# Four accumulators in turn for the first expert layer, and the written order on three engines

## The chip, the cores and the metric

The kernel runs on one core of a Trainium2 chip. The metric is the device time of one execution in microseconds (us). Three runs of the kernel before took 635.12, 649.59 and 657.23 us; their median, 649.59 us, is the time before. The profiled execution is a fourth one and took 627.53 us.

## The reference

Two blocks follow each other, all in 32-bit floats.

```
state = gamma * state + k_t v_t^T ;  y_t = scale * q_t state      # retention: batch 4, 8 heads, 768 steps, width 64
x = y as (3072 tokens, 512)
expert = argmax(x @ w_gate) ;  gate = its softmax weight           # 8 experts
out[token] = gate * ( relu(x[token] @ w1[expert]) @ w2[expert] )   # w1: 512 x 1024, w2: 1024 x 512
```

No token is dropped: each expert takes as many tokens as chose it.

## The kernel before

**Retention.** 24 steps (6 chunks of 128 positions for 4 batches) make the tokens, their logits and, chunk by chunk, the place of each token in its expert's list. Tokens are written to DRAM (`x_d`).

**Early block.** Behind the last retention step, the first 256 tokens of expert 0 go through both layers (`layer1(EARLY, ...)`, `layer2(EARLY, ...)`, lines 420 to 429), with the last logits and the placing of the last chunk (the generator `rest`) woven in between. PE's order there is the written one.

**Counts.** A matmul (`cnt`, line 434) counts the tokens of each expert. Vector instructions (lines 437 to 445) make of each count an arm number: the number of tokens is rounded up to a multiple of 32, and each multiple from 128 to 512 has code of its own, an arm.

**Jobs.** Each expert e is a job (line 469). A register on each engine that takes part holds the job's arm number; `tc.Switch` (line 479) jumps to that arm, and at the arm's end the engine jumps out again. PE and ScalarE (ACT) have arms in every job, GpSimd (POOL) in the last alone. In an arm:
- `layer1` is called for f = 0 to 7. Each call has PE gather 4 matmuls in one PSUM accumulator (`hp`), and ScalarE takes it to SBUF with a Relu (line 189). The accumulator's tag is `"sc"`, which has 2 buffers. A third call must wait until ScalarE has emptied the first accumulator.
- `turn` transposes the next job's tokens (4 tiles, tag `"tr"`, 3 buffers), and ScalarE copies them out.
- `layer2` multiplies by the second weights, tile by tile of 128 tokens (tag `"y"`, 2 buffers), ScalarE copies each result out (line 202). The last, partial tile goes first.

Between the arms, GpSimd scatters the job's 4 result tiles to the output (line 206) and gathers the tokens for the job after next (line 151), and SyncE loads the weights for the job after next (2 MB each for `w1t` and `w2t`, lines 140 and 141).

**What sets the order.** In the early block PE, and in the jobs PE and ScalarE, follow the written order (`tc.manual_schedule`). All else is placed by a scheduler: it moved all 8 register loads (`regs`, line 465) of PE and of ScalarE ahead of the first job (three of ScalarE's stand between the early block's last two Relus), moved `cnt` to the middle of the early block, and mixed GpSimd's scatters and gathers of neighbouring jobs.

**PSUM tags.** `"sc"` 2 buffers, `"tr"` 3, `"y"` 2, `"lg"` 1. In the retention part `"lg"` holds the logits, and after it `cnt`.

Of the kernel before, what the change touches and what calls it, by code (L numbers as in the profile page):

```python
# [12 lines left out]
F32 = mybir.dt.float32  # L13
I32 = mybir.dt.int32
# [3 lines left out]
ALU = mybir.AluOpType  # L18
AX = mybir.AxisListType

P = 128
# [29 lines left out]
def kernel(  # L51
# [11 lines left out]
    nc = tc.nc  # L63
    B, H, S, D = q.shape
    N, DM = out.shape
    E = w_gate.shape[1]
# [4 lines left out]
    DT = DM // P  # L71
    FT = F // P
    W = 512
    TC = W // P
    EARLY = 256
# [9 lines left out]
    def ps(tag, bufs, name):  # L85
        return psum.tile([P, 512], F32, tag=tag, name=name, bufs=bufs)
# [25 lines left out]
    def rt(shape, name, dt=F32):  # L112
        return route.tile(shape, dt, tag=name, name=name)
# [23 lines left out]
    def weights(pool, e):  # L137
        w1t = pool.tile([P, 1, DT, F], F32, tag="w1t", name="w1t")
        w2t = pool.tile([P, 1, FT, DM], F32, tag="w2t", name="w2t")
        nc.sync.dma_start(w1t, w1v[:, ds(e, 1), :, :])  # L140
        nc.sync.dma_start(w2t, w2v[:, ds(e, 1), :, :])
        return w1t, w2t

    first = ctx.enter_context(tc.tile_pool(name="first", bufs=1))
    xs2 = [first.tile([P, TC, DM], F32, tag=f"xs{i}", name=f"xs{i}") for i in range(2)]
# [3 lines left out]
    def gather(xs, idx, tiles, rows=N):  # L149
        for t in tiles:  # L150
            nc.gpsimd.indirect_dma_start(  # L151
                out=xs[:, t, :], out_offset=None, in_=x_d[0:rows, :],
                in_offset=bass.IndirectOffsetOnAxis(ap=idx[:, t : t + 1], axis=0), bounds_check=rows - 1,
                oob_is_err=False)
# [22 lines left out]
    def turn(xs, xT, tiles, evict):  # L177
        for t in tiles:
            tr = ps("tr", 3, "trs").rearrange("p (a t) -> p a t", a=DT)
            for dt in range(DT):  # L180
                nc.tensor.transpose(tr[:, dt, :], xs[:, t, ts(dt, P)], ident)
            evict(out=xT[:, :, ts(t, P)], in_=tr)

    def layer1(n, xT, w1t, hT, f):
        hp = ps("sc", 2, "hp")[:, 0:n]
        for dt in range(DT):
            nc.tensor.matmul(hp, lhsT=w1t[:, 0, dt, ts(f, P)], rhs=xT[:, dt, 0:n], start=(dt == 0),  # L187
                             stop=(dt == DT - 1))
        nc.scalar.activation(out=hT[:, f, 0:n], in_=hp, func=AF.Relu)  # L189

    def layer2(n, hT, w2t, o, t):

        m = min(n - t * P, P)
        parts = P // m if m in (P // 4, P // 2) else 1
        y = ps("y", 2, "ye")
        c = DM // parts
        for f in range(FT):
            for j in range(parts):
                nc.tensor.matmul(y[j * m : j * m + m, 0:c], lhsT=hT[:, f, t * P : t * P + m],  # L199
                                 rhs=w2t[:, 0, f, ts(j, c)], start=(f == 0), stop=(f == FT - 1))  # L200
        for j in range(parts):
            nc.scalar.copy(out=o[0:m, t, ts(j, c)], in_=y[j * m : j * m + m, 0:c])  # L202

    def scatter(o, idx, tiles):
        for t in tiles:
            done = nc.gpsimd.indirect_dma_start(  # L206
                out=out[:, :], out_offset=bass.IndirectOffsetOnAxis(ap=idx[:, t : t + 1], axis=0), in_=o[:, t, :],
                in_offset=None, bounds_check=N - 1, oob_is_err=False)

            tc.declare_no_dep(done.ins, group="scatters", reason="other rows of the output")  # L210
            tc.add_to_no_dep_group("scatters", done.ins)


    with ExitStack() as actx:
# [191 lines left out]
        for n in range(len(steps)):  # L406
# [6 lines left out]
            last, done = done, retain(n)  # L413
# [6 lines left out]
        with tc.manual_schedule(engines={mybir.EngineType.PE}):  # L420
            turn(xs2[0], xTa, range(EARLY // P), nc.vector.tensor_copy)
            for f in range(FT):
                layer1(EARLY, xTa, wa[0], hTa, f)
                if f != 4:
                    next(rest, None)
            for _ in rest:
                pass
            for t in range(EARLY // P):
                layer2(EARLY, hTa, wa[1], oa, t)
# [5 lines left out]
    ne = rt([P, E], "ne")  # L435
    arm = rt([P, E], "arm", I32)
    nc.vector.tensor_copy(ne, cnt)

    STEP, LEAST, MOST = 32, P // 32, W // 32
# [8 lines left out]
    PE, ACT, POOL = mybir.EngineType.PE, mybir.EngineType.Activation, mybir.EngineType.Pool  # L448


    mp = ctx.enter_context(tc.tile_pool(name="mp", bufs=2))
    keep2 = ctx.enter_context(tc.tile_pool(name="keep2", bufs=1))
    o2 = [keep2.tile([P, TC, DM], F32, tag=f"o{i}", name=f"o{i}") for i in range(2)]
    for t in o2:
        nc.vector.memset(t, 0.0)
    sets = [wa, weights(keep2, 1)]
    cols = [(src_i[:, ts(e, TC)], dst_i[:, ts(e, TC)]) for e in range(E)]
    HALF = EARLY // P

    gather(xs2[1], cols[0][0], range(HALF, TC))  # L460
    gather(xs2[0], cols[1][0], range(TC))
    xT = mp.tile([P, DT, W], F32, tag="xTs", name="xTs")
    turn(xs2[1], xT, range(HALF, TC), nc.vector.tensor_copy)

    def regs(e, engines):
        return {g: nc.engines[g].value_load(arm[0:1, e : e + 1], min_val=0,
                                            max_val=MOST - LEAST - (EARLY // STEP if e == 0 else 0)) for g in engines}

    for e in range(E):
        w1t, w2t = sets[e]  # L470
        skip = EARLY if e == 0 else 0
        arms = MOST - LEAST + 1 - skip // STEP
        engines = [PE, ACT] + ([POOL] if e == E - 1 else [])
        which = regs(e, engines)
        if e + 1 < E:
            xTn = mp.tile([P, DT, W], F32, tag="xTs", name="xTs")
        hT = mp.tile([P, FT, W], F32, tag="hT", name="hT", bufs=1)
        with tc.manual_schedule(engines={PE, ACT}):
            for a in tc.Switch(which, arms):
                n = STEP * (LEAST + a)  # L480
                for f in range(FT):
                    layer1(n, xT[:, :, skip:], w1t, hT, f)
                if e + 1 < E:
                    turn(xs2[e % 2], xTn, range(TC), nc.scalar.copy)
                tiles = -(-n // P)
                for t in [tiles - 1] + list(range(tiles - 1)):
                    layer2(n, hT, w2t, o2[e % 2], t)
                    if e == E - 1:
                        scatter(o2[e % 2], cols[e][1], [t])
        if e + 1 < E:  # L490
            tiles = range(TC - HALF) if e == 0 else range(TC)
            scatter(o2[e % 2], cols[e][1][:, HALF:] if e == 0 else cols[e][1], tiles)
            xT = xTn
        if e + 2 < E:
            gather(xs2[(e + 1) % 2], cols[e + 2][0], range(TC))
            sets.append(weights(first if e % 2 == 0 else keep2, e + 2))


    most = rt([P, 1], "most")
    over = rt([P, 1], "over", I32)  # L500
    nc.vector.tensor_reduce(most, ne, axis=AX.X, op=ALU.max)
    nc.vector.tensor_scalar(out=over, in0=most, scalar1=float(W), scalar2=None, op0=ALU.is_gt)
    more = nc.values_load(over[0:1, 0:1], min_val=0, max_val=1)
    with tc.If(more > 0), tc.tile_pool(name="op", bufs=1) as op:

# [51 lines left out]
        for j in range(OV):  # L557
            ev = nc.sync.value_load(whose[0:1, j : j + 1], min_val=0, max_val=E - 1)
            w1t, w2t = weights(keep2, ev)
            gather(xs2[j % 2], osrc_i[:, ts(j, TC)], range(TC))  # L560
            xT = mp.tile([P, DT, W], F32, tag="xTs", name="xTs")
            hT = mp.tile([P, FT, W], F32, tag="hT", name="hT", bufs=1)
            turn(xs2[j % 2], xT, range(TC), nc.vector.tensor_copy)
            for f in range(FT):
                layer1(W, xT, w1t, hT, f)
            for t in range(TC):
                layer2(W, hT, w2t, o2[j % 2], t)
            scatter(o2[j % 2], odst_i[:, ts(j, TC)], range(TC))
# [25 lines left out]
```

## Time and profile before

| | us |
|---|---|
| median of 3 runs (lowest, highest) | 649.59 (635.12, 657.23) |
| profiled execution, its span | 627.53, 625.7 |
| retention and early block, to the first job | about 227 |
| jobs 0 to 7, first matmul to last | 227.5 to about 610 |
| behind the last matmul | about 15 |
| PE busy | 563.8 (90%) |
| ScalarE busy | 123.8 (20%) |

The sizes of the jobs that the trace shows: job 0 runs 128 further tokens, jobs 1, 2, 5 and 7 the arm for 416, job 3 for 448, job 4 for 352, job 6 for 384. A 32-bit matmul stands in the trace as two pieces, so that a call of `layer1` is 8 pieces and two calls are the "x16" of a row. Times in rows count from the start of the span. A bracket at a row's end gives how long the engine sat idle before it and what ended that. "issue" means that the profile shows nothing that the engine waited for.

### The profile page before, as it was taken

The numbers are of one execution on the slowest core, as the hardware profiler recorded it, in microseconds if no ns is written. First come the engines' busy times: TensorE is split into PE (matmuls) and PEld (weight loads), VectorE is DVE, ScalarE is ACT, GpSimd is POOL, SyncE is SP. The second block draws the span as 40 slices with busy tenths as digits, with TensorE's granted clock in tenths as the row PEclk, the third lists the DMA queues.
The fourth block names the chain that finished last, engine by engine and source line by source line (L and its number), as shares of the span: only waits on it lengthen the run. The fifth ranks groups of instructions, "written<-read, shape, count | busy, mean of one in ns | idle before, by whom it ended". The sixth has DMA issues, their size and how long they took to land.

```text
span 625.7 us, 7784 instructions
## 1 busy us (share of the span) xinstructions
PE 563.8 (90%) x3160; PEld 371.6 (59%) x3160; DVE 108.5 (17%) x291; ACT 123.8 (20%) x245; POOL 118.8 (19%) x156
## 2 busy tenths in 40 slices
PE   4999999999999988799799989969979996999990
PEld 4988989898988664364355445436435543545540
DVE  2445555466453220000000000000000000000000
ACT  2223232323232211130012012002001201201100
POOL 8331312222220433002102200210310010000011
PEclk9997979899999999899899979999998997999996
DMA  9964647956120449513504410450550314000011
GB/s 186 211 126 124 137 129 213 316 124 159 34 89 14 132 125 381 192 47 137 186 0 170 134 75 18 170 187 0 190 183 0 139 43 147 0 4 20 4 37 50
DMA packets 96476, 72.50 MB, mean 116 GB/s; under 512 B 77946, under 2 KB 77946, under 8 KB 96384
## 3 DMA queue, kind: packets, MB, share of 16 engines
q1 hardware_dynamic: 88096, 52.46, 31.4%
q0 software_dynamic: 5120, 12.60, 5.9%
q10 hardware_dynamic: 3168, 6.29, 2.7%
q8 instruction: 48, 0.79, 0.6%
q14 instruction: 44, 0.36, 0.2%
HBM read 60.84 MB, written 14.68 MB: 121 GB/s over the span
## 4 chain that ended last, share of the span: by engine, by line
issue 56%; PE 28%; POOL 8%; DVE 4%; DMA 1%; POOLq 1%; SPq 0%; DVEq 0%
PE y L288 7%; POOL out_dram L206 4%; PE sc L260 4%; POOL xs L151 4%; PE tr L246 4%; PE y L284 4%; PE lg L308 3%; PE new L269 2%; PE hp L187 2%; PE trx L303 2%; DVE am L262 1%; DMA q<-in_q_dram 1%; DVE xT L305 0%; DVE state L276 0%; SPq L232 0%
## 5 line engine op out<-in xcount | busy, mean ns | idle before, releaser
L187 PE MATMUL hp<-xTs,w1t 128*128 128x416 f32 (+4 forms) x512 | 177.9, 509 | 31.5 <-ACT hT L189 27.8
L187 PEld LDWEIGHTS hp<-xTs,w1t 128*128 128x128 f32 x512 | 98.4, 204 | 111.4 <-issue 66.5
L199 PE MATMUL ye<-w2t,hT 128*128 128x512 f32 (+3 forms) x640 | 164.0, 455 | 0.0
L199 PEld LDWEIGHTS ye<-w2t,hT 128*128 128x128 f32 (+3 forms) x640 | 74.8, 155 | 84.2 <-issue 83.2
L206 POOL DMA_INDIRECT out_dram<-o,dst x30 | 29.8, 995 | 294.3 <-ACT o L202 236.7
L189 ACT ACTIVATE hT<-hp 128x416 f32<-128x416 f32 (+4 forms) x64 | 30.0, 480 | 178.5 <-PE hp L187 123.7
L288 PE MATMUL y<-vs,am 128*128 128x64 f32 x384 | 59.8, 276 | 1.6 <-DVE am L262 0.9
L288 PEld LDWEIGHTS y<-vs,am 128*128 128x128 f32 x384 | 54.5, 202 | 4.5 <-issue 1.8
L202 ACT COPY o<-ye 128x512 f32<-128x512 f32 (+3 forms) x40 | 17.7, 444 | 144.6 <-PE ye L199 144.3
L151 POOL DMA_INDIRECT xs<-x_d,src x30 | 30.3, 1009 | 72.6 <-PE ye L199 35.5
L262 DVE TENSOR_TENSOR am<-sc,causal 128x512 f32<-128x512 f32 x48 | 31.3, 685 | 41.7 <-PE sc L260 41.7
L284 PE MATMUL y<-stb,qT 128*128 128x128 f32 x160 | 37.6, 319 | 0.0
L260 PE MATMUL sc<-qT,kT 64*128 64x128 f32 x384 | 36.3, 300 | 0.9 <-DVE am L262 0.9
L279 POOL COPY stb<-state 64x256 f32<-64x256 f32 x40 | 19.6, 490 | 80.0 <-DVE state L276 78.9
L241 POOL TENSOR_TENSOR vs<-v,dec 128x512 f32<-128x512 f32 x24 | 25.4, 1062 | 38.5 <-PE new L269 25.7
L260 PEld LDWEIGHTS sc<-qT,kT 64*128 64x128 f32 x384 | 28.9, 196 | 5.2 <-issue 4.2
L291 ACT COPY xg<-y 128x512 f32<-128x512 f32 x24 | 14.1, 589 | 84.4 <-PE y L288 84.4
L284 PEld LDWEIGHTS y<-stb,qT 128*128 128x128 f32 x160 | 25.6, 202 | 1.3
L246 PE MATMUL tr<-ident,qs 128*128 128x128 f32 x96 | 18.5, 318 | 7.0 <-DVE qs L240 7.0
L308 PE MATMUL lg<-wg,xT 128*128 128x8 f32 x192 | 24.5, 254 | 0.3
L308 PEld LDWEIGHTS lg<-wg,xT 128*128 128x128 f32 x192 | 23.4, 192 | 1.7 <-DVE xT L305 1.2
L248 ACT COPY qT<-tr 128x512 f32<-128x512 f32 x24 | 14.1, 587 | 37.6 <-PE tr L246 37.6
(111 smaller groups left out, 340.4 us busy)
## 6 DMA issues: line engine op xcount, KB each, us to landing
w1t<-in_moe_w_dram SPq DMA_DIRECT2D x8, 2048.0 KB, 8.0
w2t<-in_moe_w_dram SPq DMA_DIRECT2D x8, 2048.0 KB, 12.0
q<-in_q_dram SPq DMA_DIRECT2D x24, 256.0 KB, 4.6
k<-in_k_dram SPq DMA_DIRECT2D x24, 256.0 KB, 3.2
v<-in_v_dram SPq DMA_DIRECT2D x24, 256.0 KB, 4.4
x_d<-xg ACTq DMA_DIRECT2D x6, 1024.0 KB, 4.4
xs<-x_d,src POOLq DMA_INDIRECT x30, 3.5
out_dram<-o,dst POOLq DMA_INDIRECT x30, 7.1
```

The source lines that it names most:

```text
L151: nc.gpsimd.indirect_dma_start(out=xs[:, t, :], out_offset=None, in_=x_d[0:rows, :], in_offset=bass.IndirectOffsetOnAxis(ap=idx[:, t : t + ...
L187: nc.tensor.matmul(hp, lhsT=w1t[:, 0, dt, ts(f, P)], rhs=xT[:, dt, 0:n], start=(dt == 0), stop=(dt == DT - 1))
L189: nc.scalar.activation(out=hT[:, f, 0:n], in_=hp, func=AF.Relu)
L199: nc.tensor.matmul(y[j * m : j * m + m, 0:c], lhsT=hT[:, f, t * P : t * P + m], rhs=w2t[:, 0, f, ts(j, c)], start=(f == 0), stop=(f == FT ...
L206: done = nc.gpsimd.indirect_dma_start(out=out[:, :], out_offset=bass.IndirectOffsetOnAxis(ap=idx[:, t : t + 1], axis=0), in_=o[:, t, :], i ...
L241: nc.gpsimd.tensor_tensor(out=vs, in0=vt, in1=inner(gk, D), op=ALU.mult)
L246: nc.tensor.transpose(tr[:, a, :], src[:, 2 * a : 2 * a + 2, :].rearrange("p h d -> p (h d)"), ident)
L260: nc.tensor.matmul(sc[j][:, a, :], lhsT=kT[r, a, :], rhs=qT[r, a, :], start=True, stop=True)
L262: nc.vector.tensor_tensor(out=am[j], in0=sc[j], in1=middle(causal[:, :], HP), op=ALU.mult)
L284: nc.tensor.matmul(y[:, ts(a, P)], lhsT=qT[:, a, :], rhs=stb[b][c % 2][:, a, :], start=True, stop=False, skip_group_check=True)
L288: nc.tensor.matmul(y[:, ts(h, D)], lhsT=am[j][:, a, :], rhs=vs[:, h, :], start=(c == 0), stop=True, skip_group_check=True)
L308: nc.tensor.matmul(lg[:, b, :], lhsT=xT[:, dt, :], rhs=wg[:, dt, :], start=(dt == 0), stop=(dt == DT - 1))
```

## The change

It does four things. `layer1` takes its accumulators in turn from 4 places: two of `"sc"`, then `"lg"`, then one of `"tr"`; this holds for the early block too, which calls the same function. The jobs, the gathers ahead of them and the first `turn` now stand in one block in which PE, ScalarE and GpSimd keep the written order. The register for job e + 1 is loaded just ahead of job e's switch (that for job 0 ahead of the first `turn`). The two vector instructions for `most` and `over` move ahead of the jobs.

```diff
+    hp_tags = [("sc", 2), ("sc", 2), ("lg", 1), ("tr", 3)]
     def layer1(n, xT, w1t, hT, f):
-        hp = ps("sc", 2, "hp")[:, 0:n]
+        hp = ps(*hp_tags[f % len(hp_tags)], "hp")[:, 0:n]
...
+    with tc.manual_schedule(engines={PE, ACT, POOL}):
+        gather(xs2[1], cols[0][0], range(HALF, TC))
+        gather(xs2[0], cols[1][0], range(TC))
+        which = regs(0)
+        xT = mp.tile([P, DT, W], F32, tag="xTs", name="xTs")
+        turn(xs2[1], xT, range(HALF, TC), nc.vector.tensor_copy)
+        for e in range(E):
...
+            if not last:
+                nxt = regs(e + 1)
...
-        with tc.manual_schedule(engines={PE, ACT}):
-            for a in tc.Switch(which, arms):
+            for a in tc.Switch(which, arms_of(e)):
                 n = STEP * (LEAST + a)
...
+            if not last:
+                scatter(o2[e % 2], cols[e][1][:, HALF:] if e == 0 else cols[e][1], range(TC - HALF if e == 0 else TC))
+                xT, which = xTn, nxt
+            if e + 2 < E:
+                gather(xs2[(e + 1) % 2], cols[e + 2][0], range(TC))
+                sets.append(weights(first if e % 2 == 0 else keep2, e + 2))
```

The order of the built programs at three places follows (a row is a line, an operation, what it writes and reads, and its size; "x" counts equal ones in a row; lines behind 183 are 2 to 9 higher in the changed kernel).

**PE, from the middle of the early block to the first job.** `found` places the last tokens, `hp` and `ye` are the early block's two layers, `trs` is the first `turn`. Before:

```order
L368 MATMUL found<-val,here 128x64
L434 LDWEIGHTS ones_b
L434 MATMUL cnt<-acc,ones_b 128x8
L187 MATMUL hp<-xTa,w1t 128x256 x8
L199 MATMUL ye<-w2t,hTa 128x512 x16
L181 MATMUL trs<-ident,xs_104 128x128 x8
L466 TENSOR_LOAD arm
L466 ISA x2
```

Seven more pairs of these two rows follow, and then the switch and the first job. Changed:

```order
L370 MATMUL found<-val,here 128x64
L189 MATMUL hp<-xTa,w1t 128x256 x8
L201 MATMUL ye<-w2t,hTa 128x512 x16
L436 LDWEIGHTS ones_b
L436 MATMUL cnt<-acc,ones_b 128x8
L471 TENSOR_LOAD arm
L471 ISA x2
L181 MATMUL trs<-ident,xs_104 128x128 x8
L471 TENSOR_LOAD arm
L471 ISA x2
L594 SWITCH_STRIDE
```

`cnt` has moved behind the whole second layer, and a register load that needs its result stands ahead of the transposes; two loads are left of eight.

**PE, the first layer in the arm for 416 tokens of job 1,** with the engines whose semaphores an instruction waits for. Before:

```order
L187 MATMUL hp_3924<-xTs_2457,w1t_2404 128x416 x3
L187 MATMUL hp_3930<-xTs_2457,w1t_2404 128x416 x4
L187 MATMUL hp_3936<-xTs_2457,w1t_2404 128x416 [waits Activation_49]
L187 MATMUL hp_3936<-xTs_2457,w1t_2404 128x416 x3
L187 MATMUL hp_3942<-xTs_2457,w1t_2404 128x416 [waits Activation_49]
```

Changed:

```order
L189 MATMUL hp_3943<-xTs_2481,w1t_2404 128x416 x3
L189 MATMUL hp_3949<-xTs_2481,w1t_2404 128x416 x4
L189 MATMUL hp_3955<-xTs_2481,w1t_2404 128x416 x4
L189 MATMUL hp_3961<-xTs_2481,w1t_2404 128x416 [waits PE_49]
L189 MATMUL hp_3961<-xTs_2481,w1t_2404 128x416 x3
L189 MATMUL hp_3967<-xTs_2481,w1t_2404 128x416 [waits Activation_49]
```

The first wait for ScalarE stood at the third call and now stands at the fifth.

**GpSimd, the end of the jobs.** `o` is a result tile, `xs` a gathered one. Before, jobs 5 and 6 and the entry of the last:

```order
L206 DMA out_dram<-o_2401,dst 3072x512 x2
L590 UNCONDITIONAL_BRANCH
L206 DMA out_dram<-o_2401,dst 3072x512 x2
L206 DMA out_dram<-o_2400,dst 3072x512 x2
L590 SWITCH_STRIDE
```

Changed, from the gathers behind job 5:

```order
L151 DMA xs_103<-x_d,src 128x512 x4
L471 TENSOR_LOAD arm
L471 ISA x2
L594 UNCONDITIONAL_BRANCH
L208 DMA out_dram<-o_2400,dst 3072x512 x4
L594 SWITCH_STRIDE
```

All four scatters of job 6 now stand ahead of the last switch, where two of them stood behind the last job; and each job's four gathers stand behind its four scatters, at the boundary between two jobs.

## Rows read from the trace of the kernel before

**Rows 1.** The page, costliest groups: out<-in, count | busy us, mean ns | idle before, releaser.

```profile
L187 PE MATMUL hp<-xTs,w1t 128*128 128x416 f32 (+4 forms) x512 | 177.9, 509 | 31.5 <-ACT hT L189 27.8
```

**Rows 2.** Waits from 240 us on: engine, line, releaser: total us, times, longest.

```profile
ACT hT L189 <- issue: 54.8, 6, 11.0
...
PE hp L187 <- issue: 2.0, 1, 2.0
```

**Rows 3.** Timeline of PE, 240 us on: start, duration, line, operation, count, idle before.

```profile
255.75 18.60 PE L187 MATMUL hp<-xTs,w1t 128*128 128x416 f32 x48 [4.39 <-ACT hT L189]
...
308.41 19.57 PE L187 MATMUL hp<-xTs,w1t 128*128 128x416 f32 x48 [4.02 <-ACT hT L189]
...
362.00 21.36 PE L187 MATMUL hp<-xTs,w1t 128*128 128x448 f32 x48 [3.56 <-ACT hT L189]
...
409.37 4.90 PE L187 MATMUL hp<-xTs,w1t 128*128 128x352 f32 x16
419.60 16.03 PE L187 MATMUL hp<-xTs,w1t 128*128 128x352 f32 x48 [5.34 <-ACT hT L189]
...
457.84 5.75 PE L187 MATMUL hp<-xTs,w1t 128*128 128x416 f32 x16
468.22 19.88 PE L187 MATMUL hp<-xTs,w1t 128*128 128x416 f32 x48 [4.63 <-ACT hT L189]
...
512.39 5.32 PE L187 MATMUL hp<-xTs,w1t 128*128 128x384 f32 x16
522.79 18.62 PE L187 MATMUL hp<-xTs,w1t 128*128 128x384 f32 x48 [5.08 <-ACT hT L189]
...
570.11 17.03 PE L187 MATMUL hp<-xTs,w1t 128*128 128x416 f32 x48 [0.74 <-ACT hT L189]
```

**Rows 4.** Timeline of ScalarE: the first Relus of jobs 4, 5, 6 and 7.

```profile
419.09 0.82 ACT L189 ACTIVATE hT<-hp 128x352 f32<-128x352 f32 x2 [8.93 <-issue]
...
467.65 0.93 ACT L189 ACTIVATE hT<-hp 128x416 f32<-128x416 f32 x2 [9.02 <-issue]
...
522.25 0.87 ACT L189 ACTIVATE hT<-hp 128x384 f32<-128x384 f32 x2 [9.08 <-issue]
...
569.54 0.93 ACT L189 ACTIVATE hT<-hp 128x416 f32<-128x416 f32 x2 [5.14 <-PE hp L187]
```

**Rows 5.** Windows: stretch, length, busy time of five engines, granted clock, DMA share, GB/s.

```profile
298.60:308.40 9.80, 5.79 (x17) 2.85 (x15) 0.00 (x0) 1.14 (x3) 3.02 (x3) 0.92 0.85 272
308.40:314.00 5.60, 5.59 (x9) 2.94 (x10) 0.00 (x0) 0.37 (x1) 0.00 (x0) 0.54 0.12 44
563.60:570.20 6.60, 5.86 (x18) 2.94 (x16) 0.00 (x0) 1.25 (x3) 0.98 (x1) 1.00 0.13 47
```

**Rows 6.** Timeline of ScalarE, the early block's last Relu, right behind three register loads.

```profile
212.36 0.38 ACT L189 ACTIVATE hTa<-hp 128x256 f32<-128x256 f32 x1 [1.35 <-issue]
```

**Rows 7.** Timeline of PE and VectorE, 200 to 228 us.

```profile
200.08 3.70 PE L187 MATMUL hp<-xTa,w1t 128*128 128x256 f32 x16
207.40 0.17 PE L434 MATMUL cnt<-acc,ones_b 128*128 128x8 bf16 x1
224.70 1.04 PE L181 MATMUL trs<-ident,xs 128*128 128x128 f32 x8
227.47 7.38 PE L187 MATMUL hp<-xTs,w1t 128*128 128x128 f32 x64 [1.73 <-DVE xTs L182]
...
200.49 0.19 DVE L320 TENSOR_TENSOR dl<-lg,mx 128x32 f32<-128x32 f32 x1
209.04 0.14 DVE L445 TENSOR_SCALAR arm<-arm 128x1 int32<-128x1 int32 x1
```

**Rows 8.** Timeline of GpSimd at the end.

```profile
610.72 0.98 POOL L206 DMA_INDIRECT out_dram<-o,dst  x1 [5.88 <-ACT o L202]
614.01 0.98 POOL L206 DMA_INDIRECT out_dram<-o,dst  x1 [2.31 <-issue]
615.30 0.98 POOL L206 DMA_INDIRECT out_dram<-o,dst  x1 [0.30 <-issue]
```

More of the change, by code (lines that the diff above doesn't have):

```diff
@@ L458, with arms_of, regs @@
     HALF = EARLY // P
[L460 to L472, printed above, removed]
-        engines = [PE, ACT] + ([POOL] if e == E - 1 else [])
[L474 to L477, printed above, removed]
-        with tc.manual_schedule(engines={PE, ACT}):
-            for a in tc.Switch(which, arms):
+    most = rt([P, 1], "most")
+    over = rt([P, 1], "over", I32)
+    nc.vector.tensor_reduce(most, ne, axis=AX.X, op=ALU.max)
+    nc.vector.tensor_scalar(out=over, in0=most, scalar1=float(W), scalar2=None, op0=ALU.is_gt)
+    def arms_of(e):
+        return MOST - LEAST + 1 - (EARLY // STEP if e == 0 else 0)
+    def regs(e):
+        engines = [PE, ACT] + ([POOL] if e == E - 1 else [])
+        return {g: nc.engines[g].value_load(arm[0:1, e : e + 1], min_val=0, max_val=arms_of(e) - 1) for g in engines}
+    with tc.manual_schedule(engines={PE, ACT, POOL}):
[5 more added lines that the diff above has]
+        for e in range(E):
+            w1t, w2t = sets[e]
+            skip = EARLY if e == 0 else 0
+            last = e == E - 1
+            if not last:
+                nxt = regs(e + 1)
+                xTn = mp.tile([P, DT, W], F32, tag="xTs", name="xTs")
+            hT = mp.tile([P, FT, W], F32, tag="hT", name="hT", bufs=1)
+            for a in tc.Switch(which, arms_of(e)):
                 n = STEP * (LEAST + a)
@@ L482 @@
                     layer1(n, xT[:, :, skip:], w1t, hT, f)
-                if e + 1 < E:
+                if not last:
                     turn(xs2[e % 2], xTn, range(TC), nc.scalar.copy)
@@ L487 @@
                     layer2(n, hT, w2t, o2[e % 2], t)
-                    if e == E - 1:
+                    if last:
                         scatter(o2[e % 2], cols[e][1], [t])
[L490 to L502, printed above, removed]
+            if not last:
+                scatter(o2[e % 2], cols[e][1][:, HALF:] if e == 0 else cols[e][1], range(TC - HALF if e == 0 else TC))
[3 more added lines that the diff above has]
+                sets.append(weights(first if e % 2 == 0 else keep2, e + 2))
     more = nc.values_load(over[0:1, 0:1], min_val=0, max_val=1)
```

## The prediction

> **What bounds the kernel now.** I read the page first, then the waits, then the timelines of PE and ScalarE at each job's start, and last the windows around one start. On the page PE is the engine that fills the span, and its first-layer matmuls are the one large group on it that waits for another engine: 27.8 us of their idle time end with the Relu of ScalarE [rows 1]. ScalarE is far from full, so the question is why it is late. The waits tell: six times, 54.8 us in all, the Relu started after idle time for which the profile shows no cause [rows 2]. The timeline places them at the first Relu of a job, 8.93 to 9.08 us after ScalarE had finished the job before [rows 4]. That is the way out of one arm, through the switch and into the next. PE makes the same way, but has work queued and loses nothing: it starts job 5 at 457.84, while ScalarE's first Relu comes at 467.65 [rows 3, 4]. With two accumulators PE does two calls of `layer1` and stops.
>
> The reader is to see two losses in each row that ends in a bracket [rows 3]. The first is the stop: 4.39 + 4.02 + 3.56 + 5.34 + 4.63 + 5.08 + 0.74 = 27.8 us over jobs 1 to 7. The second is what follows. Behind the stop of job 2 the granted clock is 0.54 for 5.6 us, which is the 1.2 GHz level for nearly all of it, while job 7, which stopped for 0.74 us only, keeps 1.00 [rows 5]. The remaining 48 pieces take 17.03 us in job 7; that is 0.355 us a piece for 416 tokens, and scaled by the columns 18.34 for 448, 14.41 for 352 and 15.72 for 384. Against these, jobs 1 to 6 take 1.57 + 2.54 + 3.02 + 1.62 + 2.85 + 2.90 = 14.5 us more [rows 3]. Together the late entry costs 42.3 us.
>
> **The change, part by part.**
>
> *Four accumulators.* PE can now do four calls before it needs a Relu. Four calls are 32 pieces: 11.35 us for 416, 9.61 for 352, 10.48 for 384. The first accumulator is free when the first Relu has ended. Counted from PE's start, today that is 9.72 + 0.41 us in job 4, 9.81 + 0.47 in job 5, 9.86 + 0.44 in job 6 (half of the row's two Relus) [rows 3, 4]. ScalarE now also loads a register ahead of the switch. Three such loads fit in 1.35 us between two Relus [rows 6], so I take 0.45 each. The accumulator is then free at 10.58, 10.73 and 10.75 us. Job 4 still stops for 1.0 us, job 6 for 0.3, job 5 has 0.6 to spare, the others more. Stops of 0.74 us kept the clock, and I charge none for these. So 42.3 us go and **1.2 us** stay.
>
> The Trainium skill ("DMA: Bandwidth & Descriptors", section "Latency and other measured facts") gives a tensor load a floor of about 600 ns, which speaks against loads between jobs. By it, the sum would be 0.6 us worse (0.15 at each of four places where a load is exposed); the row's three loads in 1.35 us are below that floor, and I keep the row.
>
> *Two of them come from other users' buffers.* In the jobs the fourth one takes turns with the transposes in `"tr"`, whose copies are done long before the next job. In the early block the third call takes `"lg"`, which VectorE reads until 200.68 (the subtraction `dl`), where PE went on at 200.08 [rows 7]. That is **0.6 us** on PE's path.
>
> *`cnt` goes behind the early block.* It shared `"lg"` and had been run in the middle, with its result ready long before it was needed. Now PE ends the second layer, runs `cnt`, and the register load behind it waits for VectorE's arm numbers. From the start of `cnt` to the last arm number took 207.40 to 209.18, 1.8 us [rows 7], and the load adds 0.45: **2.2 us** in which PE idles and its transposes wait behind the load. From the transposes to job 0 it took 2.77 us [rows 7], most of it VectorE's copies, and I leave that. Below, it can't be less than nothing, since `cnt` is now last. Above, PE's own entry into job 0 could show: at worst as long as ScalarE's entries, some 9 us from the second load, 6 us more than I count. The two idle times of about 2 us each could also cost the clock, at most job 3's 3.0 us. I take the low value, as PE's idle 1.73 us ahead of job 0 shows nothing but the copies, with a switch and eight loads just ahead.
>
> *Loads on PE between jobs.* PE's queue covers its entry in six of seven boundaries; only at job 1 it waited, 2.0 us, for nothing that is shown [rows 2]. There I add one load, **0.45 us**, elsewhere nothing: the cover is the last tile's queued matmuls. Without it, see the slower rival.
>
> *GpSimd in the written order.* Each job's gathers now wait for its scatters, at the boundary. A queue entry takes 0.98 us and about 0.3 to the next [rows 8], so eight are through in some 10 us, and the tokens are needed only when the first layer ends, 19 us or more later. At the end, two scatters of job 6 no longer stand behind the last job. GpSimd issued them at 614.01 and 615.30, the last of its own job at 610.72 [rows 8]. If the way out of the arm remains, the end comes 2.3 us sooner (616.28 against 614.01); if it follows the last scatter, 4.6. I take **2.3**. The moved `most` and `over` are two short vector instructions beside the arm numbers and cost nothing; SyncE's order is the same, and its weights come a job early.
>
> *Sum:* 627.5 - 42.3 + 1.2 + 0.6 + 2.2 + 0.45 - 2.3 = 587 us, against the profiled execution. The median is 22 us above that execution, and the rows do not show where the other runs lose it. If in stops of this kind, the changed kernel's runs lie near 587; if elsewhere, near 609. I add a third, 7 us, because the stops are what varies most within the trace (0.74 to 5.34 us): **595 us**.
>
> **The rivals.**
>
> *ScalarE comes later still.* Its entry took 5.14 us or less in job 7, with a DMA share of 0.13 around it, and 8.9 to 9.1 in jobs 4 to 6, which have a 2 MB weight load beside it (share 0.85 in job 2) [rows 4, 5]. So an entry seems to lengthen with the traffic beside it, by some 3.8 us for 2 MB. The change puts four gathers, 1 MB, at the same place, about half of them ahead of the first Relu: up to 1.9 us later. Then jobs 1, 2 and 5 stop for 1.3 us each, job 4 for 2.9, job 6 for 2.2: 7.8 us more than counted, and the clock twice, at 2.4 (the mean of the six excesses): 4.8. With the 7 us: 607 us. Against it: the gathers queue behind the scatters, so few may be moving by then.
> The Trainium skill ("Runtime: NRT & Kernel Launch", section "Instruction fetch mechanics") says that a taken branch to code outside the loaded blocks waits for a DMA fetch, and by that rule this rival gets its cause; the trace agrees in that the busier window has the longer entry, but has only one quiet one.
>
> *The way out on the other side: PE loses its lead.* A register load now stands at every boundary in PE's own stream. If PE does not get past it until the matmuls queued ahead have run, its entry starts only at the last matmul's end and is bare at all seven boundaries. Its price is ScalarE's: 54.8 + 5.14 us of entries, seven loads of 0.45, and 2.4 of clock seven times: 80 us in place of 42.3 + 2.0. With the other terms that is 627.5 + 36 + 7 = 671 us. It decides from the point at which a load holds PE for longer than the queue lasts. Against it: before job 0, eight loads and a switch stood behind the transposes, which ended at 225.74, and PE was in job 0 at 227.47 [rows 7]; 3.6 us of loads alone would not fit in between. For it: the 2.0 us at job 1 show that the lead is finite.
>
> *The buffers are not free after all.* If a copy or a reader still holds `"tr"` or `"lg"` at a job's third or fourth call, PE stops as before, and ScalarE's loads lengthen each stop: 627.5 + 0.6 + 2.2 + 0.45 + 3.2 - 2.3, or 632, some 654 beside the median. The built order speaks against it: the first wait for ScalarE in an arm is at the fifth call.
>
> **How the numbers follow.** The forecast gets 0.68, the late ScalarE 0.18, PE's lost lead 0.07, the buffers 0.05, 0.02 is left for what I don't see. The first two are faster by far more than 2% (under 636.6 us), which is about what can be told from no change here; so faster 0.87, within 2% 0.06, slower 0.07. The range takes the forecast without the added third and with the larger gain at the end (585) and some us below, as far as the other runs scatter, and above it the late ScalarE with all of the 22 us: 580 to 622.
>
> **What would show it.** Right: no idle time of PE ahead of `hp` from ScalarE over about 1 us in jobs 1 to 7; a granted clock of 1.00 through the jobs; ScalarE's first Relu as late as before and then four Relus in a row; 2 to 3 us of idle PE between `cnt` and the transposes; no scatter behind the last job's. Wrong: stops of 2 us and more at the fifth call (late ScalarE), idle PE ahead of a job's first matmul with "issue" as its cause (lost lead), or a clock that falls without a stop.

## The result and the profile after

The changed kernel took 591.57 us in the median (586.37 to 604.38, 4 runs), the kernel before beside it 642.36 us (630.09 to 657.23, 4 runs): ratio 0.9324, 95% interval 0.9153 to 0.9494. Forecast were 595 us and 580 to 622. Medians here go by all runs, ratios by the undisturbed ones of both kernels. In the profiled executions the span went from 625.7 to 587.4 us, 38.3 less.

On the page the group of first-layer matmuls now reads as follows; it answers to [rows 1], where it had 177.9 us busy and 31.5 idle.

```profile
PE 554.0 (94%) x3160; PEld 371.0 (63%) x3160; DVE 109.5 (19%) x291; ACT 122.9 (21%) x245; POOL 118.8 (20%) x156
L189 PE MATMUL hp<-xTs,w1t 128*128 128x416 f32 (+4 forms) x512 | 162.5, 478 | 2.2 <-ACT o L204 1.2
```

Both losses are gone: the idle time ahead of it, 29.3 us, and 15.4 us of the busy time, which was the same matmuls at the lower clock. In the timeline of PE each job's first layer is one row of 64 pieces where it was two with a stop between [rows 3]. Job 4 alone still stops. These are the rows of jobs 2, 4 and 6:

```profile
299.50 22.51 PE L189 MATMUL hp<-xTs,w1t 128*128 128x416 f32 x64
...
396.52 9.63 PE L189 MATMUL hp<-xTs,w1t 128*128 128x352 f32 x32
406.71 9.73 PE L189 MATMUL hp<-xTs,w1t 128*128 128x352 f32 x32 [0.57 <-issue]
...
485.45 20.80 PE L189 MATMUL hp<-xTs,w1t 128*128 128x384 f32 x64
```

ScalarE comes no sooner than before. Its timeline for jobs 2, 4 and 7 answers to [rows 4]: 9.46 and 8.89 us for the way into the arm, and then four Relus in a row (x4), because four accumulators were waiting for it.

```profile
309.74 1.75 ACT L191 ACTIVATE hT<-hp 128x416 f32<-128x416 f32 x4 [9.46 <-issue]
...
406.20 1.53 ACT L191 ACTIVATE hT<-hp 128x352 f32<-128x352 f32 x4 [8.89 <-PE hp L189]
...
534.46 0.93 ACT L191 ACTIVATE hT<-hp 128x416 f32<-128x416 f32 x2 [5.21 <-PE hp L189]
```

The windows of job 2's entry and of its whole first layer answer to [rows 5]: the DMA share is as high as it was (0.84 against 0.85), but PE is busy throughout and the granted clock is 1.00, where it was 0.54 behind the stop.

```profile
299.50:309.70 10.20, 10.20 (x31) 5.58 (x30) 0.00 (x0) 0.58 (x1) 7.04 (x7) 1.00 0.84 273
...
299.50:322.00 22.50, 22.50 (x67) 12.27 (x66) 0.00 (x0) 3.88 (x8) 8.04 (x8) 1.00 0.50 168
```

The price of the change stands between 205 and 235 us on PE; these rows answer to [rows 7]. The third early call waits 0.60 us for `dl`; `cnt` comes behind the second layer, and 2.26 us of idle time follow it, ended by VectorE's `arm`. Job 0's 64 pieces take 7.97 in place of 7.38 us.

```profile
205.47 3.69 PE L189 MATMUL hp<-xTa,w1t 128*128 128x256 f32 x16 [0.60 <-DVE dl L322]
...
230.05 0.17 PE L436 MATMUL cnt<-acc,ones_b 128*128 128x8 bf16 x1
232.48 1.86 PE L181 MATMUL trs<-ident,xs 128*128 128x128 f32 x8 [2.26 <-DVE arm L447]
234.82 7.97 PE L189 MATMUL hp<-xTs,w1t 128*128 128x128 f32 x64 [0.48 <-DVE xTs L182]
```

On GpSimd the last job's scatters are the end, with none of job 6 behind them; the last of them answers to the three of [rows 8]:

```profile
574.55 0.98 POOL L208 DMA_INDIRECT out_dram<-o,dst  x1 [5.88 <-ACT o L204]
```

Cut at rows that both timelines have, the spans compare as follows. "Changed, again" and "before, again" are second profiled executions (the last experiments below).

| stretch, us | before | before, again | changed | changed, again | expected change |
|---|---|---|---|---|---|
| start to first early `hp` (retention) | 195.27 | 220.87 | 199.92 | 200.90 | none |
| early block's first layer | 15.70 | 15.69 | 16.40 | 18.06 | +0.6 |
| its second layer's start to job 0 | 16.50 | 16.75 | 18.50 | 18.49 | +2.2 |
| job 0 to job 1 | 18.07 | 19.13 | 17.80 | 20.39 | +0.45 |
| job 1 to the last matmul's end | 364.28 | 363.64 | 321.03 | 323.39 | -41.1 |
| the tail | 15.9 | 15.9 | 13.7 | 13.8 | -2.3 |

### The profile page after: what moved, and what is told of

Same layout as the page of the kernel before. It is cut to its first block, busy times and chain, and to the rows that moved or that the text cites. A ratio compares the mean times of both kernels' runs of the same rounds, so it can differ in the third digit from the quotient of the medians.

```text
span 587.4 us, 7778 instructions
## 1 busy us (share of the span) xinstructions
PE 554.0 (94%) x3160; PEld 371.0 (63%) x3160; DVE 109.5 (19%) x291; ACT 122.9 (21%) x245; POOL 118.8 (20%) x156
## 3 DMA queue, kind: packets, MB, share of 16 engines
q10 hardware_dynamic: 3168, 6.29, 2.9%
## 4 chain that ended last, share of the span: by engine, by line
PE 54%; issue 34%; DVE 4%; POOL 3%; DMA 2%; SPq 0%; POOLq 0%; ACT 0%; DVEq 0%; ACTq 0%
PE hp L189 13%; PE ye L201 11%; PE y L290 7%; PE sc L262 5%; PE tr L248 4%; PE y L286 4%; PE lg L310 4%; PE new L271 2%; POOL xs L151 2%; PE trx L305 2%; DMA out_dram<-o,dst 1%; PE trs L181 1%; POOL out_dram L208 1%; DVE am L264 1%; DMA q<-in_q_dram 1%
## 5 line engine op out<-in xcount | busy, mean ns | idle before, releaser
L189 PE MATMUL hp<-xTs,w1t 128*128 128x416 f32 (+4 forms) x512 | 162.5, 478 | 2.2 <-ACT o L204 1.2
L189 PEld LDWEIGHTS hp<-xTs,w1t 128*128 128x128 f32 x512 | 92.8, 192 | 72.4 <-issue 55.5
L262 PE MATMUL sc<-qT,kT 64*128 64x128 f32 x384 | 37.9, 310 | 0.9 <-DVE am L264 0.9
L262 PEld LDWEIGHTS sc<-qT,kT 64*128 64x128 f32 x384 | 30.4, 205 | 5.5 <-issue 4.5
```

The lines of the kernel that those rows point to most:

```text
L262: nc.tensor.matmul(sc[j][:, a, :], lhsT=kT[r, a, :], rhs=qT[r, a, :], start=True, stop=True)
```

## The experiments

The theory: PE's stops come from ScalarE's late entry, and four accumulators bridge it; all else is worth a few us either way. Against it stood: the gain belongs to the written order or the early loads; ScalarE becomes later by what the change puts at the boundary; PE loses its lead. ScalarE's entry into a job is its idle time ahead of the job's first Relu. All stretches, stops and entries are of one profiled execution of each kernel. Besides totals I give the time from the first early `hp` to the end, which leaves the retention part out (before 430.4 us, changed 387.5).

**Accumulators alone.** Only this line of the kernel before is edited:

```
-        hp = ps("sc", 2, "hp")[:, 0:n]
+        hp = ps(*[("sc", 2), ("sc", 2), ("lg", 1), ("tr", 3)][f % 4], "hp")[:, 0:n]
```

> The kernel before with the four accumulators alone: the scheduler still orders GpSimd, and all eight loads of a register stay ahead of job 0. Theory A (two accumulators were the loss: PE stops, and the clock falls behind the stop): from the first matmul of job 1 to the last of job 7 it takes 320 to 323 us, as in the changed kernel (321.0), not 364.3 as before; no wait of PE's first layer for a Relu over 0.7 us. Job 0 starts 3 to 5 us later than before, since cnt is late here too and eight loads of 0.45 us stand behind it; two scatters still stand behind the last job (2.1 us). So the whole is 2 to 5 us above the changed kernel's. Theory B (the written order and the later loads do it): the jobs keep 360 us and more, and the whole stays within 1% of the kernel before.

Measured: 602.06 us, ratio 0.9462 (0.9344 to 0.958), 397.6 us from the first early `hp`. Jobs 1 to 7 take 321.58 us, within 0.6 us of the full change, with stops of 0.35 and 0.51 us left. So this line carries the whole gain of the jobs. But without the loads one job ahead, the late `cnt` is dear: all eight of PE's register loads stand behind it, and job 0 starts 23.41 us after the second layer's start in place of 16.50. The expectation had 3 to 5 us for that, it was 7. From the first early `hp` on it takes 10.1 us more than the full change, not 2 to 5: 4.9 for this late start, 2.0 for the tail, and most of the rest at a lower clock (1.7 us in the early block, 0.8 in job 0). The timeline of PE shows the late start in one bracket:

```profile
243.66 0.17 PE L434 MATMUL cnt<-acc,ones_b 128*128 128x8 bf16 x1
243.69 1.07 PE L181 MATMUL trs<-ident,xs 128*128 128x128 f32 x8
253.34 8.76 PE L187 MATMUL hp<-xTs,w1t 128*128 128x128 f32 x64 [8.58 <-issue]
```

**Order and loads alone.** The changed kernel with `hp_tags = [("sc", 2)]`.

> The changed kernel with two accumulators of the tag sc alone, that is the written order and the later loads without the four accumulators. Theory A: the stops are back, each longer by a load (0.45 us): jobs 1 to 7 take 364 to 370 us, PE waits 28 to 32 us for the Relu of the first layer, the granted clock falls to about 0.5 behind each; at the end 2 us less; the whole within 1% of the kernel before. Theory B: jobs near 321 us, the whole near 590 us.

Measured: 636.43 us, ratio 0.9981 (0.9924 to 1.0037): no change. The jobs take 369.20 us and the seven stops 32.8 in place of 27.8, 0.7 us a job. One register load on ScalarE now lies in each entry but job 7's; as job 7's stop is 0.41 us longer too (1.15), not all of it is the load's. What the order gains (a tail of 13.6 us, job 0 after 15.42) pays for most of that: 431.8 us from the first early `hp`. The two parts of the change are worth more together than apart: four accumulators hide the loads that the order puts on ScalarE, and the early loads spare the wait that the accumulators bring by moving `cnt`.

**Three accumulators.** `hp_tags = [("sc", 2), ("sc", 2), ("lg", 1)]`.

> The changed kernel with three accumulators (two of sc, one of lg). Theory A by its numbers: the first accumulator is free some 10.7 us after PE's start, three calls last 8.5 us for 416 tokens, 9.1 for 448, 7.2 for 352, 7.9 for 384: stops of about 2.2, 1.5, 3.5 and 2.9 us, 15 us over jobs 1 to 6 and none in job 7, so 336 us for the jobs if the clock holds; if each stop costs the clock as before (2.4 us), 350 us. The rival that any stop past PE's second call costs the same as before says 364.

Measured: 627.04 us, ratio 0.988 (0.9741 to 1.0019; two runs), 408.2 us from the first early `hp`, jobs 339.71. The stops of jobs 1 to 7 are 0.52, 2.03, 1.30, 4.05, 2.40, 2.86 and 0 us against 2.2, 2.2, 1.5, 3.5, 2.2, 2.9 and 0 expected. So the size of a stop can be counted from the calls that PE can run ahead, but for job 1, where PE itself comes later. The 339.71 us lie between the 336 expected for a clock that holds and the 350 for one that falls at each stop, and the rival's 364 is out; the total is not told apart from the kernel before. The clock is not as simple. Of these rows of PE (jobs 2, 4 and 5) the first and last have their 40 pieces at the upper level behind stops of 2.03 and 2.40 us; behind 4.05 they take 15.16 us where 12.1 would do (job 4's clean 9.63 + 9.73 for 64, less the 7.26 of its first 24). Behind job 6's 2.86 us it fell too.

```profile
333.70 14.23 PE L189 MATMUL hp<-xTs,w1t 128*128 128x416 f32 x40 [2.03 <-issue]
...
435.32 15.16 PE L189 MATMUL hp<-xTs,w1t 128*128 128x352 f32 x40 [4.05 <-issue]
...
483.63 14.23 PE L189 MATMUL hp<-xTs,w1t 128*128 128x416 f32 x40 [2.40 <-issue]
```

**The early block on its old buffers.** The changed kernel, in which the early block's calls take turns between the two `"sc"` buffers only:

```
-    def layer1(n, xT, w1t, hT, f):
-        hp = ps(*hp_tags[f % len(hp_tags)], "hp")[:, 0:n]
+    def layer1(n, xT, w1t, hT, f, tags=hp_tags):
+        hp = ps(*tags[f % len(tags)], "hp")[:, 0:n]
...
-                layer1(EARLY, xTa, wa[0], hTa, f)
+                layer1(EARLY, xTa, wa[0], hTa, f, hp_tags[0:2])
```

> The changed kernel, but the early block keeps the two accumulators of sc, so that lg is free and cnt stands in the middle of that block again. If my two prices there are right (0.7 us for the wait on the logits' reader, 2.0 us for the register load that waits for cnt), the early block takes 15.7 us from its first hp to its first ye (before 15.70, changed 16.40), and 16.5 from there to the first hp of job 0 (before 16.50, changed 18.50): 2.7 us less, too little for the times to tell. The rival: the load itself, not cnt, holds PE up, and the second stretch stays near 18.5.

Measured: 598.41 us in the median (580.83 to 611.86, 4 runs). The early block's first layer takes 15.69 us, `cnt` is back in its middle, and job 0 comes 15.42 us after the second layer's start, 3.1 less than in the changed kernel and 1.1 less than in the one before, since only two loads are on the way. So it was `cnt`, not the load, that held PE up. Much of the gain is given back one job later: PE, sooner done with job 0, waits 2.12 us for its own entry into job 1, and behind that wait the 64 pieces take 24.28 in place of 22.59 us. From the first early `hp` it is 386.4 us, 1.1 less than the changed kernel.

**No second weights beside the entry.** In the changed kernel only the first-layer weights of jobs 2 to 7 are loaded:

```
-                sets.append(weights(first if e % 2 == 0 else keep2, e + 2))
+                pool = first if e % 2 == 0 else keep2
+                w1n = pool.tile([P, 1, DT, F], F32, tag="w1t", name="w1t")
+                nc.sync.dma_start(w1n, w1v[:, ds(e + 2, 1), :, :])
+                sets.append((w1n, w2t))
```

> The changed kernel, with the second-layer weights of jobs 2 to 7 not loaded: the two sets of experts 0 and 1 are used again and again, so no 2 MB of second weights move while ScalarE makes its way from one arm into the next; all matmuls, gathers and scatters stay (the output is that of other weights). My theory in the prediction: an entry grows with the traffic beside it (5.2 us at the quiet job 7, about 9.2 us at jobs 2 to 6). Then the entries of jobs 2 to 5, which have lost their second-weight load, fall to 5.2 to 6.5 us. Rival: the length is that of the code path and has nothing to do with traffic; then all of them stay at 8.6 to 9.5 us. Under both, PE's jobs take about 320 us, as no stop is left to be saved but 0.6 us.

Measured: ScalarE's entries into jobs 1 to 6 are 5.87, 5.96, 5.83, 5.93, 5.88 and 5.96 us, against 9.22, 9.46, 9.52, 8.89, 9.50 and 8.65 in the changed kernel; job 7's is 5.23 against 5.21. The window of job 2's entry has a DMA share of 0.32 where it was 0.84. Timeline of ScalarE, job 2, and the window:

```profile
313.35 0.93 ACT L191 ACTIVATE hT<-hp 128x416 f32<-128x416 f32 x2 [5.96 <-PE hp L189]
```

```profile
306.60:313.40 6.80, 6.80 (x21) 3.77 (x20) 0.00 (x0) 0.64 (x2) 4.51 (x5) 1.00 0.32 121
```

So the weight load lengthens an entry by 3.3 us; the rival of a fixed code path is out. The jobs take 320.19 us against 321.03, and the 0.84 us are job 4's stop of 0.57 us and 0.27 for starting again behind it: behind four accumulators an entry of 5.9 or of 9.2 us is nearly the same. The list of DMA queues also tells where in the entry the time goes. These are the first 5 us of ScalarE's way into job 2 (queue, kind: packets, MB, share of 16 engines), from 300.3 us on in the changed kernel, where queue q1 carries the weights:

```profile
q1 hardware_dynamic: 583, 1.19, 86.7%
q14 instruction: 1, 0.01, 0.7%
```

and from 307.4 us on in this run, where q1 has nothing:

```profile
q14 instruction: 3, 0.02, 1.2%
```

Without the weights the second packet of instructions comes 2.8 us into the way, with them 6.4 us, so the added time lies between the first two packets. That q14 is ScalarE's I read from the times alone: in jobs 1 to 7 of both runs its first packet comes 0.3 to 0.6 us behind ScalarE's last instruction. How the weights hold the packet back is not shown. The Trainium skill ("Runtime: NRT & Kernel Launch", section "Instruction fetch mechanics") has a taken branch wait for a DMA fetch when its target is not among the pages already loaded. The trace agrees with that by these packets.

**Eight more loads on PE ahead of each switch but the last's.**

```
+                for _ in range(8):
+                    nc.engines[PE].value_load(arm[0:1, e + 1 : e + 2], min_val=0, max_val=arms_of(e + 1) - 1)
                 xTn = mp.tile([P, DT, W], F32, tag="xTs", name="xTs")
```

> The changed kernel with eight more register loads on PE ahead of each job's switch but the last's, their values unused: the doubling of the suspected cost in PE's stream. My theory: PE's queue runs ahead of its matmuls, so a load at a boundary lies beside queued matmuls; eight loads at 0.45 us are 3.6 us, and PE's entry of some 9 to 10 us has about 3 us to spare at jobs 2 to 6, so 0 to 1 us of idle PE ahead of the first matmul there and some 3.6 us more at job 1, where there was no cover (1.19 us, so about 4.8): the span 4 to 9 us longer. Rival (PE loses its lead at a load): PE would idle 9 us and more at each boundary, over 60 us in all. If loads cost nothing at all at any boundary, the lead is longer than I think.

Measured: 616.23 us in one run, 420.1 from the first early `hp`, 32.6 more than the changed kernel; I had expected 4 to 9. These are the first-layer rows of PE in jobs 0, 1, 2 and 5:

```profile
234.89 10.31 PE L189 MATMUL hp<-xTs,w1t 128*128 128x128 f32 x64 [6.29 <-issue]
...
257.79 24.28 PE L189 MATMUL hp<-xTs,w1t 128*128 128x416 f32 x64 [3.95 <-issue]
...
309.54 24.15 PE L189 MATMUL hp<-xTs,w1t 128*128 128x416 f32 x64 [3.02 <-issue]
...
461.28 22.59 PE L189 MATMUL hp<-xTs,w1t 128*128 128x416 f32 x64 [2.67 <-issue]
```

At job 0 they are bare: 6.29 us of idle time in place of 0.48, so some 0.73 us a load, not 0.45. At jobs 2 to 6 idle times of 2.63 to 3.02 us appear; by 0.73 each the eight are 5.8 us, so some 3 us of them are hidden, as expected. The price was wrong, the cover right. At job 1, where I had expected no cover, they cost 2.76 us (3.95 in place of 1.19), no more than elsewhere. The lead is not lost, which would have cost 9 us a boundary; but it is short. The rest is the clock: six of the seven rows of jobs 0 to 6 run 1.5 to 2.3 us longer behind their wait; job 5's alone does not, behind 2.67 us.

**Four more loads on ScalarE ahead of each switch but the last's**, in the same place with `ACT` and `range(4)`.

> The changed kernel with four more register loads on ScalarE ahead of each job's switch but the last's, their values unused. My theory: ScalarE's first Relu of a job comes 1.8 us later (0.45 each; 2.4 us by the floor of 600 ns that the Trainium skill states), so entries of about 11 us in place of 9.2; PE then stops at the fifth first-layer call for about 1.0 to 1.3 us in jobs of 416 tokens, 0 to 0.3 with 448, 2.5 to 2.8 with 352 and about 2.3 with 384; the jobs take some 8 us more in all, the clock stays at its upper level as no stop is over 2.9 us. Rival: the loads lie beside something else in ScalarE's way from arm to arm (code loading, a wait) and cost nothing: entries stay at 9.2 and no stop over 0.6 us appears.

Measured: 607.82 us in one run, 399.2 from the first early `hp`. The entries of jobs 2 to 6 are 10.68 to 11.92 us, in the mean 11.31 against 9.20: 0.53 us a load. As the means of other executions with one load there range from 9.14 to 9.51 (the run with eight more on PE, 9.73, left aside), a load is 0.45 to 0.54 us. The stops are back although there are four accumulators: 1.41 us in job 2, 2.71 in job 4, 1.94 in job 5 and 2.38 in job 6, none in jobs 1, 3 and 7. Jobs 4, 6 and 3 are as expected, of the jobs of 416 tokens one is near it, one above and job 1 without. The jobs take 332.92 us, 11.9 more than in the changed kernel, where I had expected 8. That the stop is ScalarE's entry less what PE can run ahead is shown by this run and by the one with three. The clock was not as expected, as the rows of PE for jobs 4, 5 and 6 show: 32 clean pieces are 9.73, 11.44 and 10.59 us, so it fell behind 2.71 and 1.94 us, and held behind 2.38. The expectation that no stop under 2.9 us costs the clock was wrong already by the run with three accumulators (2.86).

```profile
417.59 11.12 PE L189 MATMUL hp<-xTs,w1t 128*128 128x352 f32 x32 [2.71 <-ACT hT L191]
...
464.19 13.13 PE L189 MATMUL hp<-xTs,w1t 128*128 128x416 f32 x32 [1.94 <-ACT hT L191]
...
514.48 10.59 PE L189 MATMUL hp<-xTs,w1t 128*128 128x384 f32 x32 [2.38 <-ACT hT L191]
```

**GpSimd back with the scheduler.**

```
-    with tc.manual_schedule(engines={PE, ACT, POOL}):
+    with tc.manual_schedule(engines={PE, ACT}):
```

> The changed kernel with only PE and ScalarE held to the written order, GpSimd back with the scheduler as before. My theory: the order on GpSimd is worth only what lies behind the last matmul: two scatters of job 6 stand behind the last job's again, and the time from the last matmul to the end goes from 13.75 back to about 15.8 us; the jobs take 320 to 323 us either way, and ScalarE's entries stay at 9.2 us. Rival (gathers at the boundary lengthen ScalarE's entry, as my slower case had it): entries shorten by 0.4 us or more once the scheduler is free to place them elsewhere.

Measured: 594.92 us in one run, 391.7 from the first early `hp`; the tail is 15.92 us again, with two scatters of job 6 behind the last job's (the timeline of GpSimd):

```profile
578.08 0.98 POOL L208 DMA_INDIRECT out_dram<-o,dst  x1 [5.88 <-ACT o L204]
581.25 0.98 POOL L208 DMA_INDIRECT out_dram<-o,dst  x1 [2.19 <-issue]
582.54 0.99 POOL L208 DMA_INDIRECT out_dram<-o,dst  x1 [0.30 <-issue]
```

The jobs take 322.73 us. The entries of jobs 2 to 6 are 9.50 us in the mean, not shorter than 9.20. The written order on GpSimd is worth those 2.2 us at the end, and no cost to ScalarE shows.

**Second executions of both, and a fifth accumulator.** The changed kernel and the one before ran once more unedited. The last kernel is the one with the early block on its old buffers, and besides:

```
-    hp_tags = [("sc", 2), ("sc", 2), ("lg", 1), ("tr", 3)]
+    hp_tags = [("sc", 2), ("sc", 2), ("lg", 1), ("tr", 3), ("tr", 3)]
```

> The changed kernel once more, for a second profiled execution and beside the next one. My theory by now: what differs between executions of one kernel sits in the retention part ahead of the expert layers (its end between 195 and 221 us in the profiles so far, with granted clocks of 0.83 to 0.98 there), while the jobs repeat to a few us: from job 1's first matmul to the last one's end 320 to 324 us again, whatever the total. Rival (the reason I gave for the added third): the stops vary from run to run; then the jobs' stretch differs by 5 us and more.

> The kernel before, for a second profiled execution. Under the theory that the runs' spread sits in the retention part, its stops come to about 28 us again (25 to 31) and its jobs take 364 us from job 1's first matmul to the last one's end (360 to 368); the rest of any difference from 627.5 us lies ahead of the first early matmul. Under the rival the stops' sum moves by 5 us and more with the total.

> The changed kernel with a fifth accumulator in the jobs' turn (the second "tr" buffer) and the early block back on the two "sc" buffers, which lets the written order run cnt mid-block again. Five calls are 14.2 us for 416 tokens, 12.0 for 352, 13.1 for 384, all more than the 10 to 11 us after which the first accumulator is free: no stop at any job (0.57 us in the changed kernel's job 4), early block 15.7 in place of 16.4 us, last early matmul to job 0 about 2 to 3 us less: 3 to 4 us less than the changed kernel in the stretch from the first early matmul to the end, which is 0.5 to 0.6% and may not be told apart in the total, since the retention part varies by more. Rival: the transposes at a job's end, which use the same three "tr" buffers, now wait for Relus of that layer, and give it back: idle PE ahead of the 16 transposes of 0.5 us and more a job.

Measured: the changed kernel 597.46 us (593.26 to 603.46, 6 runs), ratio 0.9402 (0.9336 to 0.9468); before 640.77 (627.38 to 657.69, 11 runs); the profiled execution of before 653.79 us, 26.3 above the first one. Nearly all of that, 25.6 us, lies ahead of the first early `hp`; the stops sum to 28.75 us against 27.8, the jobs to 363.64 against 364.28. In the retention part PE runs the same matmuls in the same order in both. The same four transposes (`tr<-ident,k`) start at 54.33 us in the first and at 75.09 in the second, so 20.8 us are lost by then. A window of that stretch and the matmuls of line 269 in it (count | busy us, mean ns), for the first execution and then for the second:

```profile
25.00:50.00 25.00, 23.49 (x219) 20.32 (x217) 13.66 (x34) 6.22 (x12) 7.69 (x10) 0.93 0.73 136
L269 PE MATMUL new<-vs,k 128*64 128x64 f32 x48 | 2.1, 228 | 0.0
```

```profile
25.00:50.00 25.00, 25.00 (x142) 21.98 (x142) 6.06 (x11) 3.51 (x6) 4.07 (x6) 1.00 0.37 76
L269 PE MATMUL new<-vs,k 128*64 128x64 f32 x32 | 2.2, 321 | 0.0
```

In the second PE is busy throughout and slower: 142 matmuls in place of 219, and 321 ns for one that takes 228. That looks like the lower clock, yet the granted clock of the window reads 1.00, so this column does not account for the stretch, and the cause there stays open. Later the column goes with the pace:

```profile
100.00:195.00 95.00, 91.36 (x930) 84.36 (x928) 50.83 (x140) 27.71 (x50) 21.11 (x30) 0.98 0.54 148
```

```profile
100.00:195.00 95.00, 91.76 (x883) 84.62 (x883) 49.55 (x123) 27.65 (x49) 21.49 (x33) 0.87 0.59 159
```

At 0.87 in place of 0.98 PE gets through 883 matmuls there, not 930. Over all thirteen profiled executions the part ends between 194.4 and 220.9 us. The rival, stops that vary by 5 us and more from run to run, is not seen in these two executions of either kernel. The changed kernel's two executions differ by 7.6 us, 1.0 of it in the retention part and 6.6 behind it: 1.7 in the early block, 2.6 between job 0 and job 1, 2.4 in the jobs. So its jobs keep within the 320 to 324 us of my theory (323.39), but not all of the difference lies in the retention part: behind the waits around job 0 the second execution lost more of the clock than the first.

The fifth accumulator: 605.07 us (587.13 to 607.34, 7 runs), ratio 0.9287 (0.9184 to 0.9389). Its profiled execution has a retention part of 220.64 us. Behind that it takes 384.9 us, against 387.5 and 394.1 of the changed kernel: 2.6 and 9.2 less, with no stop in any job, as this row of job 4 shows, and no idle time ahead of the jobs' transposes.

```profile
415.66 19.10 PE L189 MATMUL hp<-xTs,w1t 128*128 128x352 f32 x64
```

The intervals of the two ratios overlap, so it is not shown to be faster in the total. From the first early `hp` on it is the least of all profiled executions here, though the changed kernel's own two lie 6.6 us apart there.

## Why the prediction was right, step by step

- **The late entry and its 42.3 us: right.** The jobs lost 43.25 us in place of 41.1. Of the sum's terms, the stops went from 27.8 to 0.57 us in the first execution and 1.23 in the second, all in job 4 (1.2 forecast, in jobs 4 and 6). Behind them some 16 us went, not 14.5. The difference is the stop's own edge, which I had not seen: job 7's two rows sum to 5.75 + 17.03 = 22.78 us without a loss of clock, and in one piece the layer takes 22.51, so each stop avoided is worth 0.27 us more (six of them 1.6).
- **0.45 us a load: right in kind, too low for PE.** ScalarE pays 0.45 to 0.54, PE some 0.73 where the loads are bare. I had read the price from the 1.35 us of idle time alone [rows 6]; with the 0.39 us of the Relu before, it is 1.74 us from start to start, so the row allows up to 0.58 a load. The Trainium skill's floor of 600 ns ("DMA: Bandwidth & Descriptors", section "Latency and other measured facts") lies between the two engines and is no floor for ScalarE here. For the one or two loads of this change it made little difference.
- **0.6 us in the early block:** 0.70.
- **2.2 us for the late `cnt`:** 2.0. My upper bound, an entry of PE's own, was not seen: the 8.58 us of the accumulators alone are mostly loads. There VectorE's last arm number was ready at 246.36 us and PE was in job 0 at 253.34; of these 7.0 us eight loads at 0.73 are 5.8. One job ahead, there are only two loads. The clock, which I left out there, did cost 0.6 us in job 0 and 2.1 in the second execution (7.97 and 9.48 us against 7.38).
- **0.45 us at job 1: not borne out.** PE's wait there went from 2.05 us (1.49 in the second execution of before) to 1.19 in one execution and 2.27 in the other; the rest of the stretch from job 0 to job 1 is job 0's clock, counted above. In most runs the wait is the shorter the longer job 0 takes: 1.85 to 2.30 us behind 7.38 us, 1.18 to 1.55 behind 7.9 to 9.8. The changed kernel's second execution (2.27 behind 9.48) and the run with eight more loads do not fit. Behind the longer wait the clock fell, which I had not counted: job 1's first layer takes 22.59 us behind 1.19 us of idle time, 24.28 behind 2.27.
- **2.3 us at the end:** 2.1, and back without the written order on GpSimd.
- **7 us for the runs' spread: its reason was wrong.** I gave a third of the 22 us because the stops vary most within the trace. They hardly vary between executions (27.8 and 28.75 us). Of the 26.3 us between the two executions of before, 25.6 are the retention part's, which I had not looked at. That 595 us lies near the medians of 591.57 and 597.46 is luck.
- **587 us for the profiled execution, measured 589.08: near in part by luck.** Behind the first early `hp` the change saved 42.9 us, where my terms sum to 40.2; the retention part, in which it changes nothing, happened to be 4.7 us longer.
- **The rivals.** ScalarE later because of gathers: the entries of jobs 2 to 6 grew by 0.44 us in the mean (8.76 to 9.20), not by up to 1.9. Not even these 0.44 us are shown to come from the gathers or the load: the accumulators alone, with neither at the boundary in the new way, gave 9.19. Its premise, that traffic lengthens an entry, is shown for the 2 MB of weights; the gathers follow at the end of the entry, behind four scatters. PE's lost lead: no idle time ahead of jobs 2 to 7; one load fits in the cover of some 3 us. The held buffers: not seen in the jobs of any run.

## What to carry to other kernels

Where two engines go through the same branch, the one with work queued arrives first; count for how long it can run without the other (calls times pieces times the row's time a piece) and compare that with the time until the other has freed the first buffer. Here two calls of 4.9 to 6.2 us, against some 10 us, cost 43 us; four, 9.6 to 12.1 us, cost next to nothing. Buffers that lie idle at that moment are the cheapest way to lengthen it, but a borrowed buffer carries its old user's place in the order with it: look for what is moved (here `cnt`), and what stands behind that.

Before an addition is made for the spread of the runs, take a second profile of the same kernel and see in which stretch it lies. Check the granted clock of a stretch against the time that one matmul takes there.

## What the runs showed of the hardware

- The way from one arm of the switch to the next takes ScalarE 5.1 to 5.3 us in job 7, which loads no register, 5.8 to 6.0 with one register load, and 8.6 to 9.6 in jobs 2 to 6 of the changed kernel's two executions, with that load and 2 MB of weights beside it. With the weights, the second packet of instructions on the way into job 2 comes after 6.4 us, without them after 2.8.
- The clock behind idle time of PE ahead of or within a first layer: it held in all rows with 1.55 us or less in jobs 1 to 7, and fell in all with 3.5 us or more. Between, the length does not tell: it held behind 2.03, 2.38, 2.40 and 2.67 us, and fell behind 1.94, 2.12, 2.27, 2.30, 2.63, 2.71, 2.86 (three rows) and 3.02. In kernels with two accumulators it held behind 1.85 and 2.05 for the 16 pieces up to the next stop. What else decides stays open.
- The matmuls of the retention part get 0.98 and 0.87 of the clock from 100 to 195 us in two executions of one and the same program; ahead of that one execution ran matmuls of 228 ns in 321 ns, and the granted clock did not show it. Why was not found.
